# Exchanging two of the four first weight pieces between two DMA queues, one of them now between activation chunks

## The chip, the cores and the metric

The kernel runs on one core of one Trainium2 chip. The metric is the device time of one execution in microseconds (us); lower is better. All runs below are with a granted TensorE clock of 1.00. "Span" is the time that the profiler sees between the first and the last instruction; it is about 1.75 us shorter than the device time of the same run. In the profile PE is TensorE (matmuls and transposes), DVE is VectorE, ACT is ScalarE and POOL is GpSimd; "SP's queue" and "ScalarE's queue" hold the transfers that SyncE (SP) and ScalarE issue.

## The reference

The program is one transformer block of 2048 tokens by 1024 channels in bf16: a layer norm, an attention with 32 heads in four segments of 512 tokens, then a gated MLP. Only its first lines matter here:

```python
q = layernorm(x) @ wq ;  k = layernorm(x) @ wk ;  v = layernorm(x) @ wv
# then, per segment of 512 tokens: softmax(q k^T) v with a causal mask, plus a memory term; o @ wo; MLP
```

## The kernel before

Nothing can be computed until the first data have come, so the start of the kernel is laid out by hand. Segment 0 is four chunks of 128 tokens, x0 to x3 (256 KB each). The left half of `wv` is loaded in four pieces of 256 input rows (256 KB each), called pieces 0 to 3 here. V needs all four pieces; the pieces are consumed in the order of accumulation.

```python
for tc in range(4):
    x_load(tc)                       # SP queue: x0, x1, x2, x3
wv_piece(3, sp)                      # SP queue: piece 3
sp.dma_start(WK[:, :, 0:256], ...)   # then the other weights
# ... cut ...
for k in range(3):
    wv_piece(k, act)                 # ScalarE queue: pieces 0, 1, 2
```

In segment 0 the norm is done late. Chunks are only centered before the projection, V is scaled by 1/std when it leaves PSUM (the memory that TensorE writes its results to), and for Q and K the four chunks' 1/std are broadcast by TensorE (the tile `RSB`) and multiplied on. `act_mean` is a sum on ScalarE, `center` a subtraction on VectorE, `pe_Th` eight transposes on TensorE with two copies out of PSUM, `act_var` a sum of squares on ScalarE; `act_var` with its `rstd0`, and `aggr0`, each end in a pair of small GpSimd instructions. `v_pair(t, lo, hi)` is the V matmuls of chunk t with the 128-row blocks lo to hi, two blocks to a piece.

```python
v_pair(0, 0, 2)                 # chunk 0, piece 0
c1 = center(1, MEAN[1][:])
stats0(0, 0)
pe_Th(1, c1, dve, dve)
act_mean(2)                     # ScalarE: waits for x2
v_pair(0, 2, 4)                 # piece 1
v_pair(1, 0, 4)
v_pair(0, 4, 6)                 # piece 2
c2 = center(2, MEAN[2][:])
act_mean(3)                     # ScalarE: waits for x3
c3 = center(3, MEAN[3][:])
act_var(1)                      # chunk 1, but behind act_mean(2), act_mean(3) on ScalarE
rstd0(1)
stats0(0, 1)
aggr0(0)
pe_Th(2, c2, dve, act)
act_var(2)
rstd0(2)
v_pair(1, 4, 6)
v_pair(0, 6, 8)                 # piece 3
v_pair(1, 6, 8)
stats0(3, 0)
pe_Th(3, c3, dve, act)
stats0(3, 1)
aggr0(3)
# ... RSB; V of chunk 2; first K projection; TensorE broadcast of RSB; first Q projection ...
```

Of the kernel before, what the change touches and what calls it, by code (L numbers as in the profile page):

```python
# [257 lines left out]
def bass_sequential_preLN__memory_aug_infini_attn__mixer_gmlp__prompt_kernel(  # L258
# [17 lines left out]
    pe, act, dve, pool, sp = R.pe, R.act, R.dve, R.pool, R.sp  # L276
# [118 lines left out]
    def x_load(tc, eng=sp):  # L395
        eng.dma_start(XCH[tc % 4][:], x2d[tc * 128:(tc + 1) * 128, :])

    def wcols(ap, lo, hi):
        return ap[:, lo:hi].rearrange("(c p) n -> p c n", p=128)

    def wv_piece(k, eng):
        eng.dma_start(WV[0][:, 2 * k:2 * k + 2, :],
                      A_wv[k * 256:(k + 1) * 256, 0:512].rearrange("(c p) n -> p c n", p=128))

    for tc in range(4):
        x_load(tc)
    wv_piece(3, sp)
    sp.dma_start(WK[:, :, 0:256], wcols(A_wk, 0, 256))
    sp.dma_start(BETAB[:], A_beta.partition_broadcast(128))
    sp.dma_start(WQ[:, :, 0:256], wcols(A_wq, 0, 256))  # L410
# [7 lines left out]
    act.activation(RDM[:, 0, 0:1], MHALF[:], ACTF.Exp)  # L418
    pool.iota(IOT[:], [[1, 128]], base=0, channel_multiplier=-1)
    pool.memset(WV[0][:, 0, 0:16], 0.0)  # L420
    for k in range(3):
        wv_piece(k, act)
    pool.memset(V[:, :, :, 32:34], 1.0)
    pool.memset(BLK[:], 1.0)
# [509 lines left out]
    for tb in range(4):  # L934
# [9 lines left out]
        for tcl in range(4):  # L944
            tc = 4 * tb + tcl
# [38 lines left out]
```

## Time and profile before

| | before |
|---|---|
| device time | 795.58 us median of 3 (795.53 to 796.05) |
| span of the profiled run (a separate run of 796.20 us) | 794.5 us |
| TensorE busy | 784.4 us, 99% of the span |
| start of the first K projection | 13.98 us |
| start of the first Q projection | 16.16 us |

The first lines of the page give the span and the busy time of each engine (time, share, instructions):

```profile
span 794.5 us, 13030 instructions
...
PE 784.4 (99%) x5570; PEld 378.3 (48%) x5662; DVE 378.6 (48%) x741; ACT 296.7 (37%) x349; POOL 166.7 (21%) x329
```

TensorE is busy nearly always, so what can be won by moving loads lies in the start. The chain of waits, cut to the first 30 us, follows the last instruction back to what released it (start, duration, what):

```profile
0.79 0.91 ACT L209
...
1.74 6.50 DMA wv<-in_A_wv_dram
...
8.28 4.14 PE ps L209 x30
...
12.47 9.03 PE ps L209 x49
```

One load, a `wv` piece, is charged 6.50 us, and from its landing on TensorE runs almost without a stop. The timeline of TensorE shows what it did meanwhile (start, busy time, engine, source line, operation, output<-inputs, count; in brackets how long it was idle and what ended that):

```profile
6.78 0.62 PE L209 MATMUL ps<-ident,lno 128*128 128x128 bf16 x8
8.28 1.95 PE L209 MATMUL ps<-wv,xnT 128*128 128x512 bf16 x8 [0.88 <-DMA wv<-in_A_wv_dram]
10.07 0.61 PE L209 MATMUL ps<-ident,lno 128*128 128x128 bf16 x8
10.52 1.46 PE L209 MATMUL ps<-wv,xnT 128*128 128x512 bf16 x6
11.81 0.61 PE L209 MATMUL ps<-ident,lno 128*128 128x128 bf16 x8
12.47 1.67 PE L209 MATMUL ps<-wv,xnT 128*128 128x512 bf16 x7
13.98 1.89 PE L209 MATMUL ps<-xnT,wk 128*128 128x512 bf16 x8
15.71 0.61 PE L209 MATMUL ps<-ident,rsb 128*128 128x128 bf16 x8
16.16 1.89 PE L209 MATMUL ps<-xnT,wq 128*128 128x512 bf16 x8
```

The transposes of chunk 1 end at 7.40, then TensorE idles 0.88 us for piece 1. These are the lines the change was aimed at. "ident,lno" is a chunk's transposes, "xnT,wk" and "xnT,wq" the first K and Q projections, and "ident,rsb" the broadcast of the 1/std values. The GpSimd timeline shows their making, four pairs of instructions, of which the first and the very last instruction are shown:

```profile
10.70 0.19 POOL L209 TENSOR_SCALAR rs<-rs 128x1 f32<-128x1 f32 x1 [8.66 <-ACT junk L209]
...
13.90 0.56 POOL L209 TENSOR_TENSOR rsw<-rs,mhalf 128x1 f32<-128x1 f32 x1
```

The last ends at 14.46. On ScalarE the sum of x2 starts at 7.01:

```profile
7.01 1.06 ACT L209 ACTIVATE junk<-xch 128x1024 bf16<-128x1024 bf16 x1 [1.19 <-DMA xch<-in_A_x_dram]
...
9.38 1.15 ACT L209 ACTIVATE junk<-xch,mean 128x1024 bf16<-128x1024 bf16 x1
```

### The profile page before, as it was taken

How to read it: one execution, taken by the hardware profiler on the slowest of the kernel's cores; microseconds unless marked ns; L12 is line 12 of the kernel's file. 1: busy time of each engine (PE TensorE's matmuls, PEld its weight loads, DVE VectorE, ACT ScalarE, POOL GpSimd, SP SyncE). 2: the span in 40 equal slices, each digit the busy share in tenths (PEclk: the TensorE clock that was granted, in tenths of full speed). 3: DMA queues.
4: the chain of work that ended last, by engine and by line, in shares of the span. 5: the costliest groups of instructions: out<-in, count | busy, mean ns of one | idle time of the engine just before them, and what ended most of it. 6: DMA issues, size and time to landing. Idle time of an engine off the chain costs nothing.

```text
span 794.5 us, 13030 instructions
## 1 busy us (share of the span) xinstructions
PE 784.4 (99%) x5570; PEld 378.3 (48%) x5662; DVE 378.6 (48%) x741; ACT 296.7 (37%) x349; POOL 166.7 (21%) x329
## 2 busy tenths in 40 slices
PE   8999999999999999999999999999999999999998
PEld 3444455555554455455544444444444444444444
DVE  5585689579854766744561000053233323323332
ACT  6778877887787674233333333100000000000000
POOL 2665555556553331100230000000000000000000
PEclk9999999999999999999999999999999999999999
DMA  9544556364414425411116000740260143011002
GB/s 305 169 138 81 93 81 127 82 108 90 99 28 121 113 68 142 117 47 54 54 54 132 1 1 0 223 89 7 79 133 1 33 113 73 1 59 54 1 7 86
DMA packets 125002, 64.83 MB, mean 82 GB/s; under 512 B 94992, under 2 KB 113936, under 8 KB 124944
## 3 DMA queue, kind: packets, MB, share of 16 engines
q1 hardware_dynamic: 124128, 63.20, 32.9%
q8 instruction: 44, 0.72, 0.4%
q10 hardware_dynamic: 816, 0.79, 0.3%
q14 instruction: 14, 0.11, 0.0%
HBM read 32.51 MB, written 8.39 MB: 51 GB/s over the span
## 4 chain that ended last, share of the span: by engine, by line
PE 93%; DVE 5%; issue 1%; DMA 1%; ACT 0%; DVEq 0%
PE ps L209 93%; DVE stats L209 1%; DMA wv<-in_A_wv_dram 1%; DVE hch L209 1%; DVE otok L209 0%; DVE pqk L209 0%; DVE lno L209 0%; DVE ta L209 0%; DVE etmp L209 0%; DVE rd L209 0%; DVE mv L209 0%; DVE rdm L209 0%; ACT e L209 0%; ACT L209 0%; DVE upd L209 0%
## 5 line engine op out<-in xcount | busy, mean ns | idle before, releaser
L209 PE MATMUL ps<-wspT,z 128*128 128x512 bf16 x878 | 193.1, 379 | 0.9
L209 ACT ACTIVATE e<-ps 128x2048 bf16<-128x2048 f32 (+1 forms) x96 | 152.6, 1590 | 41.7 <-PE ps L209 41.5
L209 PEld LDWEIGHTS ps<-wspT,z 128*128 128x128 bf16 x896 | 87.7, 98 | 105.7
L209 DVE TENSOR_TENSOR tmpg<-ps,brow 128x512 f32<-128x512 f32 x56 | 38.7, 691 | 197.0 <-DMA brow<-in_B_b_sp_dram 104.0
L209 POOL TENSOR_SCALAR_AFFINE_SELECT e<-e 128x512 bf16<-128x512 bf16 x128 | 90.6, 720 | 132.4 <-ACT e L209 132.4
L209 PE MATMUL ps<-win,hnT 128*128 128x448 bf16 x512 | 98.3, 352 | 0.0
L209 PE MATMUL ps<-w_out,yT 128*128 128x512 bf16 (+2 forms) x453 | 96.9, 372 | 0.5
L209 PE MATMUL ps<-hnT,win 128*128 128x512 bf16 x439 | 96.2, 379 | 0.5
L209 PEld LDWEIGHTS ps<-win,hnT 128*128 128x128 bf16 x512 | 49.7, 98 | 46.4 <-issue 0.2
L209 PEld LDWEIGHTS ps<-w_out,yT 128*128 128x128 bf16 x462 | 44.7, 98 | 52.4
L209 PEld LDWEIGHTS ps<-hnT,win 128*128 128x128 bf16 x448 | 43.8, 98 | 52.8
L209 PE MATMUL ps<-xnT,wk 128*128 128x512 bf16 x233 | 59.6, 380 | 1.2
L209 PE MATMUL ps<-wv,xnT 128*128 128x512 bf16 x255 | 59.4, 380 | 1.2 <-DMA wv<-in_A_wv_dram 0.9
L209 ACT ACTIVATE z<-ps 128x448 bf16<-128x448 f32 x60 | 32.5, 543 | 69.4 <-PE ps L209 69.4
L209 PE MATMUL ps<-wo,oT 128*128 128x512 bf16 x254 | 57.7, 380 | 0.1
L209 ACT ACTIVATE z1T<-ps 128x512 bf16<-128x512 f32 x56 | 33.4, 597 | 63.3 <-PE ps L209 63.3
L209 DVE TENSOR_TENSOR fin<-fin,ps 128x512 bf16<-128x512 bf16 (+2 forms) x33 | 22.2, 672 | 71.2 <-DMA fin<-out_dram 38.7
L209 PE MATMUL ps<-xnT,wq 128*128 128x512 bf16 x226 | 54.0, 379 | 1.6
L209 DVE BATCH_NORM_STATS2 zst<-z 128x6 f32<-128x448 bf16 x64 | 38.9, 620 | 30.1 <-ACT z L209 30.1
L209 PEld LDWEIGHTS ps<-v,e 128*128 128x128 bf16 x1280 | 38.8, 96 | 14.0 <-issue 6.5
L209 PE MATMUL ps<-v,e 128*128 128x33 bf16 x1280 | 42.2, 178 | 0.0
L209 DVE TENSOR_TENSOR yT<-tmpg,z1T 128x512 bf16<-128x512 f32 x56 | 38.8, 692 | 1.9
(88 smaller groups left out, 603.9 us busy)
## 6 DMA issues: line engine op xcount, KB each, us to landing
xch<-in_A_x_dram SPq DMA_DIRECT2D x16, 256.0 KB, 3.7
xr<-in_A_x_dram SPq DMA_DIRECT2D x16, 256.0 KB, 4.0
out_dram<-hch SPq DMA_DIRECT2D x16, 256.0 KB, 2.4
fin<-out_dram SPq DMA_DIRECT2D x16, 256.0 KB, 2.8
out_dram<-fin SPq DMA_DIRECT2D x31, 128.0 KB, 1.7
win<-in_B_w_in_dram SPq DMA_DIRECT2D x4, 896.0 KB, 5.0
w_out<-in_B_w_out_dram SPq DMA_DIRECT2D x1, 3584.0 KB, 12.4
win<-in_B_w_in_dram SPq DMA_DIRECT2D x3, 1024.0 KB, 5.1
```

What stands on the lines that cost most here:

```text
L209: ins = getattr(e, op.name)(*op.args, **op.kw)
```

## The change

The intent is to have piece 1 earlier: it leaves ScalarE's queue, where it stood behind piece 0, and takes the third place on SP's queue, ahead of x2 and x3. In exchange piece 3 leaves SP's queue, and pieces 2 and 3 follow piece 0 on ScalarE's. The same bytes are moved by the same number of transfers.

```diff
-    for tc in range(4):
-        x_load(tc)
-    wv_piece(3, sp)
+    x_load(0)
+    x_load(1)
+    wv_piece(1, sp)
+    x_load(2)
+    x_load(3)
     sp.dma_start(WK[:, :, 0:256], wcols(A_wk, 0, 256))
 ...
-    for k in range(3):
+    for k in (0, 2, 3):
         wv_piece(k, act)
```

## The prediction

> **What bounds it now.** TensorE: 784.4 us busy of a span of 794.5 (the page, part 1), granted clock 1.00, and the chain of waits is 93% TensorE. In the first 30 us the chain names one load: 0.79 us of start-up, then 6.50 us of "DMA wv<-in_A_wv_dram" from 1.74 to 8.23, then TensorE almost without a gap until 24.8. The timeline: TensorE ends the transposes of x chunk 1 at 7.40 and starts the next V matmuls at 8.28, idle 0.88 us, waiting for the second w_v piece.
>
> **Landings before, us from the trace's semaphore records.** On SP's queue x0 3.7, x1 4.59, x2 6.93, x3 8.05, w_v piece 3 9.80; on ScalarE's queue pieces 0, 1, 2 at 5.11, 8.23, 9.58. Packets of both queues run in the same windows and move 300 to 380 GB/s together from 2.5 us on: they are full, so the change can only reorder bytes. The Trainium skill ("DMA: Bandwidth & Descriptors", section "Issuing engines are not separate DMA queues") says so: both queues interleave on the same 16 engines. Each gets about half.
>
> **What the change does.** It adds no bytes. Piece 1 is issued third on SP (about 1.72 us, against 1.74 on ScalarE before; an issue takes 0.40 to 0.49 us on either). It takes x2's place in SP's order; x2 takes x3's, x3 takes piece 3's; pieces 2 and 3 move up one place on ScalarE's. Estimates from the landings above: piece 1 at 6.9 (gain 1.3), piece 2 at 7.9, x2 at 8.0 (loss 1.1), x3 at 9.2 (loss 1.1), piece 3 at 9.6.
>
> **Critical path.** Piece 1 is then there before 7.40, so the 0.88 us idle should vanish; the eight V matmuls (0.22 us each) end near 9.2 instead of 10.07. But then the transposes of chunk 2 need its mean: x2 8.0, ScalarE sum 1.06 + 0.19, VectorE centering 0.49, so they start at 9.8, a new TensorE gap of about 0.6 us. Next, VectorE's centering of chunk 3 (9.38 before) goes to about 10.5, and behind it in program order the chunk 0 statistics and the chunk 2 copy (10.63 before, near 11.75 after). The V matmuls of chunk 2 need that copy: ready near 12.1, while TensorE reached them at 12.2 before. So of 0.88 us some 0.6 returns as the new gap and most of the rest in a second one. The first K projection (13.98 before) should start between 13.7 and 14.4. From there TensorE is full and carries the shift, about nothing, to the end. At most 0.3 us gained, at worst about 0.8 lost.
>
> **Predicted: 795.6 us, 794.9 to 796.5 (8 in 10). Faster by over 2%: 0; within 2%: 1.0; slower by over 2%: 0.** 2% is 16 us.
>
> **What would show it.** Right: no TensorE wait on wv near 8; one of 0.4 to 0.8 us for lno before the chunk 2 transposes; ScalarE's sum of x2 starting near 8.1, not 7.01; centering of chunk 3 later by about 1 us; K projection within 0.4 us of 13.98. Wrong: piece 1 landing after 7.4, or x2 landing before 7.4 (then up to 0.6 us is really gained).
>
> **What would make it wrong.** Arbitration that isn't even between queues (piece rows are 1 KB, x rows 2 KB); one slow DMA engine setting landings (piece 1's sixteen part landings spread from 6.26 to 8.23); x3 landing past 9.4, which delays everything behind its centering; and run-to-run spread, 0.5 us in three runs.

## The result

The changed kernel took 796.89 us (median of 4, 796.57 to 797.64), the kernel before 795.82 us (median of 4, 795.53 to 796.10). The ratio is 1.0015 with a 95% interval of 0.9998 to 1.0032. (The ratio and its interval are taken from the fast runs themselves, and are not quite the ratio of the medians quoted.) By the threshold of 2% that is the same time. But it lies above the predicted range, and the experiments show where the loss comes from, and that it is mostly smaller than in these four runs.

The page of the changed kernel, same lines:

```profile
span 795.9 us, 13122 instructions
...
PE 789.8 (99%) x5662; PEld 378.2 (48%) x5662; DVE 378.7 (48%) x741; ACT 296.7 (37%) x349; POOL 167.2 (21%) x329
```

(TensorE's busy sum is not comparable to a few microseconds: the earlier trace has 5570 matmul records, this one 5662, so some were missing there.) The chain of waits no longer goes through a `wv` piece but through an x chunk, and it now visits every engine:

```profile
2.18 7.05 DMA xch<-in_A_x_dram
...
9.32 1.16 ACT junk L209 x2
...
10.50 1.16 ACT junk L209 x2
...
11.69 0.49 DVE lno L209
...
13.94 0.24 POOL rs L209
...
14.26 0.57 POOL rsw L209
...
16.14 0.57 POOL rsw L209
...
16.73 0.18 DVE rsb L209
...
17.16 12.85 PE ps L209 x86
```

It reads: x2 lands at 9.23; ScalarE sums x2, then x3; VectorE centers chunk 3; statistics; the GpSimd pairs; the `rsb` cast; and only at 17.16 does TensorE broadcast 1/std. (One step of it is doubtful, see below.) TensorE's timeline, line for line as before:

```profile
6.64 0.62 PE L209 MATMUL ps<-ident,lno 128*128 128x128 bf16 x8
8.21 1.90 PE L209 MATMUL ps<-wv,xnT 128*128 128x512 bf16 x8 [0.94 <-DMA wv<-in_A_wv_dram]
11.05 0.62 PE L209 MATMUL ps<-ident,lno 128*128 128x128 bf16 x8 [0.94 <-DVE lno L209]
11.50 1.46 PE L209 MATMUL ps<-wv,xnT 128*128 128x512 bf16 x6
12.80 0.61 PE L209 MATMUL ps<-ident,lno 128*128 128x128 bf16 x8
13.36 1.90 PE L209 MATMUL ps<-wv,xnT 128*128 128x512 bf16 x8
15.10 1.89 PE L209 MATMUL ps<-xnT,wk 128*128 128x512 bf16 x8
17.16 0.62 PE L209 MATMUL ps<-ident,rsb 128*128 128x128 bf16 x8 [0.17 <-DVE rsb L209]
17.61 1.89 PE L209 MATMUL ps<-xnT,wq 128*128 128x512 bf16 x8
```

Three waits are to be seen. In this run the one for piece 1 is still there (0.94 us). A new one of 0.94 us stands before the transposes of chunk 2 ("<-DVE lno"). And another, labelled 0.17 us, stands before the broadcast of `rsb`. The last is worth more than its label, since the label counts from the modelled end of the last matmul: from the start of the K projection to that of the broadcast it is 17.16 - 15.10 = 2.06 us here, and 15.71 - 13.98 = 1.73 us before. GpSimd and ScalarE show why it is there:

```profile
13.02 0.19 POOL L209 TENSOR_SCALAR rs<-rs 128x1 f32<-128x1 f32 x1 [10.97 <-ACT junk L209]
...
16.14 0.56 POOL L209 TENSOR_TENSOR rsw<-rs,mhalf 128x1 f32<-128x1 f32 x1
```

```profile
9.32 1.06 ACT L209 ACTIVATE junk<-xch 128x1024 bf16<-128x1024 bf16 x1 [3.25 <-DMA xch<-in_A_x_dram]
...
11.68 1.15 ACT L209 ACTIVATE junk<-xch,mean 128x1024 bf16<-128x1024 bf16 x1
```

GpSimd's first pair waited for the variance of chunk 1. That needs neither x2 nor x3, but stands behind both of their sums in ScalarE's program order. So the variance started at 11.68 instead of 9.38, and the last of the four pairs ended at 16.70 instead of 14.46. The chain of waits names VectorE's statistics before the second pair (13.94), but GpSimd was busy with the first pair until 13.86, and the statistics that the second pair needs were ready at 13.02. In experiment 6 below, where the first pair goes earlier, the second starts at 11.98, while the statistics named here run on until 12.78. So it was the first pair that held it.

When each load landed is in the trace's semaphore records. A load counts as landed when the last of its sixteen parts has arrived. In us, with the median of the sixteen parts in brackets:

| | x2 | x3 | piece 1 | piece 2 | piece 3 |
|---|---|---|---|---|---|
| before | 6.93 (5.70) | 8.05 (7.34) | 8.23 (6.41) | 9.58 (8.27) | 9.80 (8.59) |
| changed | 9.23 (7.17) | 10.37 (8.49) | 8.16 (5.85) | 8.42 (6.34) | 10.59 (8.48) |

By the median part the queues did what was asked: pieces 1 and 2 came 0.56 and 1.93 us earlier, x2 and x3 1.47 and 1.15 later. But a tile is usable only with its last part, and in this run that came about 2 us behind the median part from the third transfer on (8.16 - 5.85 = 2.31, 9.23 - 7.17 = 2.06, 10.37 - 8.49 = 1.88). Two of the sixteen parts were late each time (piece 1's at 7.31 and 8.16, x2's at 8.54 and 9.23, x3's at 9.66 and 10.37), the other fourteen had landed by 6.74, 7.78 and 9.08. That looks like one or two DMA engines that fell behind and stayed behind, but it isn't shown, since the records don't name the engine.

The Trainium skill ("DMA: Bandwidth & Descriptors", section "Why a DMA increments its semaphore by 16 and not by 1") says that a transfer runs on up to sixteen engines that finish independently and that only the full count means that all has landed. The trace agrees: sixteen part landings per load, spread over as much as 2.8 us for piece 1 (5.37 to 8.16) and 3.2 us for piece 3 (7.43 to 10.59).

### The profile page after: what moved, and what is told of

Same layout as the page of the kernel before. It is cut to its first block, busy times and chain, and to the rows that moved or that the text cites. A ratio compares the mean times of both kernels' runs of the same rounds, so it can differ in the third digit from the quotient of the medians.

```text
span 795.9 us, 13122 instructions
## 1 busy us (share of the span) xinstructions
PE 789.8 (99%) x5662; PEld 378.2 (48%) x5662; DVE 378.7 (48%) x741; ACT 296.7 (37%) x349; POOL 167.2 (21%) x329
## 4 chain that ended last, share of the span: by engine, by line
PE 98%; DMA 1%; DVE 0%; POOL 0%; ACT 0%; SPq 0%; issue 0%; ACTq 0%
PE ps L209 98%; DMA xch<-in_A_x_dram 1%; ACT junk L209 0%; POOL rsw L209 0%; SPq L209 0%; DVE stats L209 0%; POOL rs L209 0%; DVE lno L209 0%; DVE rsb L209 0%; DVE fin L209 0%; DVE xnT L209 0%; DVE mv L209 0%; ACTq L208 0%
## 5 line engine op out<-in xcount | busy, mean ns | idle before, releaser
L209 PE MATMUL ps<-xnT,wq 128*128 128x512 bf16 x256 | 60.5, 379 | 0.0
```

What stands on the lines that cost most here:

```text
L209: ins = getattr(e, op.name)(*op.args, **op.kw)
```

## The experiments

Twelve kernels ran, each five times, in three sessions on three chips (1 to 4, 5 to 8, 9 to 12), beside nine runs of the kernel before in each session. All passed the comparison with the reference, also the two that compute something wrong (experiments 2 and 7), whose error it doesn't see.

One measure made a difference of half a microsecond readable. In all fourteen traces (before, changed, twelve experiments) the span minus the start of the first Q projection is 778.25 to 778.34 us. So whatever these kernels differ in, and also what one run differs from another, arose before the first Q projection. Its start, called Q here, is the number to explain.

Theory X: x2 and x3 lose a place on SP's queue, and their chain through ScalarE, VectorE and GpSimd then holds TensorE. Rival W: the `wv` pieces in their new places hold it. Rival S: it is chance in the slowest DMA engine, and the order costs nothing.

### 1. The changed kernel again

The loops are written out; the instructions are the same.

> The changed kernel, again, for its time over five rounds and for a second trace. Theory X (x chunks 2 and 3 land one place later and the chunk 2 and 3 chain then holds TensorE): 0.6 to 1.3 us slower than before, x2 landing after 8.0, first K projection starting 14.6 to 15.2. Rival S (the profiled run only caught a slow DMA engine; the order costs nothing): times within 0.3 us of before, first K projection near 14.0.

Measured: 796.73 us (796.15 to 797.12), before 796.36 (795.67 to 796.55), ratio 1.0004 (0.9991 to 1.0018). x2 landed at 8.48, piece 1 at 7.42, Q was 16.84. TensorE's timeline:

```profile
7.47 1.90 PE L209 MATMUL ps<-wv,xnT 128*128 128x512 bf16 x8
10.29 0.62 PE L209 MATMUL ps<-ident,lno 128*128 128x128 bf16 x8 [0.93 <-DVE lno L209]
...
16.39 0.62 PE L209 MATMUL ps<-ident,rsb 128*128 128x128 bf16 x8 [0.15 <-DVE rsb L209]
```

This time the wait for piece 1 is gone (the V matmuls start at 7.47). The waits for lno and rsb are there again. So those two belong to the change; the wait for piece 1 in the first trace came of its late last part. The time lies 0.37 us above before by the medians and the first K projection started at 14.34: both fall between what theory X said (0.6 to 1.3, 14.6 to 15.2) and what rival S said (within 0.3, near 14.0), and the interval doesn't exclude a difference of zero.

### 2. Nothing early waits for x2 and x3 (wrong result)

The transfers stay as in the change. The norm's early work on chunks 2 and 3 reads chunks 0 and 1:

```diff
-    act_mean(2)
+    act_mean(2, 0)              # reads XCH[0] in place of XCH[2]
-    c2 = center(2, MEAN[2][:])
+    c2 = center(2, MEAN[2][:], src=0)
# ... the same for act_var(2) and, with chunk 1's data, for chunk 3 ...
```

> The changed kernel with the first norm's work on chunks 2 and 3 reading chunks 0 and 1 instead (wrong result on purpose), so nothing early waits for x2 and x3; all transfers stay. Theory X: the 0.94 us TensorE wait for lno and the later centering of chunk 3 go, first K projection at 13.7 to 14.2, time within 0.3 us of before or up to 0.4 below. Rival W (the w_v pieces in their new places are what holds TensorE): the loss stays, K projection near 15, time 0.6 to 1.3 above before.

Measured: 795.32 us (794.98 to 795.47) against 796.36, ratio 0.9988 (0.9975 to 1.0000). Q was 14.93. TensorE no longer stops between the V matmuls and Q:

```profile
7.07 1.94 PE L209 MATMUL ps<-wv,xnT 128*128 128x512 bf16 x8
8.84 0.61 PE L209 MATMUL ps<-ident,lno 128*128 128x128 bf16 x8
...
12.75 1.89 PE L209 MATMUL ps<-xnT,wk 128*128 128x512 bf16 x8
14.48 0.61 PE L209 MATMUL ps<-ident,rsb 128*128 128x128 bf16 x8
14.93 1.89 PE L209 MATMUL ps<-xnT,wq 128*128 128x512 bf16 x8
```

Without the x chain the moved pieces are worth 1.04 us against the kernel before (medians) and 1.41 us against the changed kernel. That is more than expected. Here neither piece sets Q any more: by the sums derived below, piece 1 (6.80) would give 14.73 and piece 2 (7.64) 14.22, and the chain of waits goes back to x0. Rival W falls: with the same transfers, it is the dependence on x2 and x3 that makes the change lose.

### 3. Displacement alone

```diff
-    x_load(2); x_load(3); wv_piece(3, sp)
+    wv_piece(3, sp); x_load(2); x_load(3)      # ScalarE keeps pieces 0, 1, 2
```

> Displacement alone: SP carries x0, x1, piece 3, x2, x3 and ScalarE pieces 0, 1, 2 as before, so x2 and x3 lose a place but piece 1 gains nothing. Theory X: x2 lands 8.0 to 9.3, as slow as the change (0.6 to 1.3 us above before). Rival W: x is harmless, time within 0.3 us of before.

Measured: 796.19 us (796.06 to 796.57) against 796.36, ratio 1.0000 (0.9987 to 1.0012). A miss for the size in theory X: no loss is seen in the times, which by themselves fit rival W's forecast here. The trace says that the mechanism was there all the same: x2 landed at 8.19, the chain of waits runs through x2, ScalarE and GpSimd to `rsb` as in the changed kernel, and Q was 16.55, 0.39 later than in the trace of before. With x2 at 8.2 the chain is hardly longer than what TensorE waited for pieces 1 and 2 anyway. The cost is not a fixed number; it is the difference of two nearly equal paths.

### 4. Piece 1 on SP, x2 in its old place on ScalarE's queue

```diff
-    x_load(2); x_load(3); wv_piece(3, sp)       # SP, behind x0 and x1
+    wv_piece(1, sp); x_load(3); wv_piece(3, sp)
-    wv_piece(0, act); wv_piece(1, act); wv_piece(2, act)
+    wv_piece(0, act); x_load(2, act); wv_piece(2, act)
```

> Piece 1 in SP's third place, as in the change, but x2 takes piece 1's old place on ScalarE's queue and x3 and piece 3 stay where they were. Theory X: x2 lands about 8.2 (one and a quarter late, not two), x3 8.0 as before, piece 2 at 9.6 as before and therefore still the gate of the fifth V matmul of chunk 0; K projection 13.9 to 14.5, time between before and 0.6 above. If an early piece 1 is worth something by itself: up to 0.5 us below before.

Measured: 795.92 us (795.84 to 796.46) against 796.36, ratio 0.9998 (0.9985 to 1.0010). x2 landed at 7.33, x3 at 8.70, piece 2 at 8.88, Q was 15.87. It is no loss, and by the medians a gain of 0.44 that the interval doesn't confirm. The chain goes through x3 here, so this version too ends on the x chain. The landings were misjudged: x2 was expected near 8.2, piece 2 at 9.6 and the first K projection at 13.9 or later; it started at 13.38.

### 5. The kernel before again

The loop is written out; the instructions are the same.

> The kernel before, written out differently, instruction for instruction the same: for a second trace of it and for the size of the noise. Time within 0.4 us of the runs of before beside it. From the traces so far, span minus start of the first Q projection is 778.25 to 778.34 in every kernel, so all differences arise before it. Expected here: Q projection start 15.6 to 16.5, set by the w_v pieces (piece 1's landing + 7.9), and 778.3 again.

Measured: 796.23 us (795.73 to 796.41) against 796.31 (795.92 to 796.63) for the same program in the same session. The ratio is 0.9998 (0.9986 to 1.0011), which is what nothing looks like here. Q was 16.19. In this trace the chain ran through piece 2 (landed at 9.61), not piece 1. In the first trace of before both give the same Q, so an early piece 1 alone could not have gained: piece 2 stood right behind it.

### 6. The changed kernel with the variance of chunk 1 moved forward

```diff
+    act_var(1)
+    rstd0(1)
     act_mean(2)
     ...
     c3 = center(3, MEAN[3][:])
-    act_var(1)
-    rstd0(1)
```

> The changed kernel with the variance sum of chunk 1 (ScalarE) and its rsqrt (GpSimd) moved in program order ahead of the sum of chunk 2, which waits for x2. Theory X2 (after the change the path runs x2, two ScalarE sums, the variance of chunk 1 queued behind them, then four rsqrt pairs back to back on GpSimd, then the TensorE broadcast of them): GpSimd's first pair starts near 7.4, no TensorE wait for rsb, Q projection at x2's landing + 7.9 instead of + 8.36, time 0.3 to 0.6 us below the changed kernel. If only the transposes of chunk 2 matter: no change of time beyond 0.2.

Measured: 796.17 us (795.82 to 796.39) against 796.31, ratio 0.9998 (0.9986 to 1.0011). x2 landed at 8.12 and Q was 16.15, that is 8.03 after it, against 8.38, 8.36 and 8.36 in the three traces of the changed kernel. GpSimd's first pair, and TensorE:

```profile
7.11 0.19 POOL L209 TENSOR_SCALAR rs<-rs 128x1 f32<-128x1 f32 x1 [5.07 <-ACT junk L209]
```

```profile
9.93 0.62 PE L209 MATMUL ps<-ident,lno 128*128 128x128 bf16 x8 [0.47 <-DVE lno L209]
...
15.70 0.61 PE L209 MATMUL ps<-ident,rsb 128*128 128x128 bf16 x8
```

The pair starts at 7.11, the wait for `rsb` is gone, and from K to the broadcast it is 1.72 us, as before the change. The wait for lno stays, as it must with x2 late. So the order of one ScalarE instruction behind two sums it doesn't need was worth 0.33 us. The ratio to before is 0.06% lower than in experiment 1; that comparison goes across two sessions.

### 7. The kernel before, not waiting for x2 and x3 (wrong result)

The edit of experiment 2 on the kernel before.

> The kernel before with the first norm's work on chunks 2 and 3 reading chunks 0 and 1 (wrong result on purpose). Theory X: before the change x2 and x3 are in good time (x2's landing 6.93 + 8.36 is 15.3, the w_v pieces give 16.1), so nothing changes: Q projection 15.6 to 16.5, time within 0.3 us of before. If the reading of other chunks speeds things by itself: 0.5 us or more below, and then e2_nox proves less.

Measured: 796.25 us (795.94 to 796.65) against 796.31, ratio 1.0000 (0.9988 to 1.0013), Q 15.89. Before the change the x chain is off the path, and the edit by itself gains nothing. That makes experiment 2 count.

### 8 and 11. The kernel before with another TensorE order

```diff
-    v_pair(0, 2, 4)
-    v_pair(1, 0, 4)
-    v_pair(0, 4, 6)
+    v_pair(1, 0, 2)             # needs piece 0 only
+    v_pair(0, 2, 4)
+    v_pair(1, 2, 4)
     ...
     pe_Th(2, c2, dve, act)
+    v_pair(0, 4, 6)
```

> The kernel before, transfers unchanged, with TensorE's order changed: chunk 1's first two V matmuls, which need only piece 0, go ahead of the wait for piece 1, and the transposes of chunk 2 ahead of the matmuls of piece 2. Theory: fills about 0.45 us of the 0.88 us wait, Q projection at about 15.7, time 0.3 to 0.5 us below before. If the wait merely moves to piece 2 (9.58): within 0.15 us of before.

> e8_peorder again, for a second trace and more spans: the earlier transfers with TensorE's reordered start. Expected 0.4 to 0.7 us below before, Q projection 15.3 to 16.0.

Measured: 795.62 us (795.35 to 796.24) against 796.31, ratio 0.9994 (0.9981 to 1.0008), Q 15.41; and again 795.90 us (795.55 to 796.19) against 796.11 (795.37 to 796.96), ratio 0.9998 (0.9985 to 1.0010), Q 15.77. From the first of the two traces:

```profile
7.59 1.47 PE L209 MATMUL ps<-wv,xnT 128*128 128x512 bf16 x6 [0.30 <-DVE xnT L209]
8.89 0.61 PE L209 MATMUL ps<-ident,lno 128*128 128x128 bf16 x8
...
15.41 1.89 PE L209 MATMUL ps<-xnT,wq 128*128 128x512 bf16 x8
```

The wait for piece 1 is filled with work that was ready. Q is 0.4 to 0.8 us earlier than in the two traces of before; the times lie 0.69 and 0.21 us below it by the medians, and both intervals hold 1. The gain of the second run is smaller than expected (0.4 to 0.7).

### 9. The changed kernel a third time

The kernel of experiment 1.

> The changed kernel a third time, for a third trace and five more spans beside the repaired versions. Expected: 0.3 to 0.9 us above before; Q projection at x2's landing + 8.36, x2's last part landing 8.2 to 9.2, a TensorE wait for rsb of 0.1 to 0.2. If a fourth of its runs are as fast as before's median, the loss is mostly one of chance in the slowest DMA engine.

Measured: 796.41 us (796.08 to 796.58) against 796.11, ratio 1.0003 (0.9990 to 1.0015). x2 landed at 8.14, Q was 16.50. Of its five runs two (796.08 and 796.11) reach before's median of 796.11, more than a fourth, so by the mark set beforehand the loss is mostly one of chance in the slowest DMA engine. The chain itself is there: x2 landed just before the expected 8.2 to 9.2, and Q is its landing + 8.36, as expected.

### 10. The changed kernel, repaired

Experiment 6, and the two matmuls of chunk 1 with piece 2 go ahead of the wait for chunk 2:

```diff
     v_pair(0, 4, 6)
+    v_pair(1, 4, 6)
     ...
     pe_Th(2, c2, dve, act)
     ...
-    v_pair(1, 4, 6)
```

> The changed kernel, repaired for late x chunks: variance of chunk 1 ahead of the sum of chunk 2 (as in e6_var1), and two V matmuls of chunk 1 with piece 2 ahead of the transposes of chunk 2, to fill the wait for them. Theory: Q projection at x2's landing + 7.5, that is 15.7 to 16.2, time 0.2 to 0.6 us below before.

Measured: 796.26 us (795.85 to 796.81) against 796.11, ratio 1.0001 (0.9987 to 1.0015). A miss. x2 landed at 8.59 and Q was 16.62, 8.03 after it and not 7.5. The time saved before the chunk 2 transposes came back one step later: TensorE then waited 0.38 us for the copy of chunk 2, which stands behind the centering of chunk 3 in VectorE's order, and that waits for ScalarE's sum of x3. It is the step that the prediction had named as "a second one". The wait on TensorE's timeline:

```profile
12.71 1.90 PE L209 MATMUL ps<-wv,xnT 128*128 128x512 bf16 x8 [0.38 <-DVE xnT L209]
```

### 12. Transfers in the order of need

```diff
-    x_load(2); x_load(3); wv_piece(3, sp)
+    x_load(2); wv_piece(1, sp); x_load(3)       # ScalarE: pieces 0, 2, 3
```

The TensorE order is that of experiment 8, with `v_pair(1, 4, 6)` still directly after `v_pair(0, 4, 6)`; `act_var(1)`, `stats0(0, 1)`, `aggr0(0)` and `pe_Th(2)` go ahead of chunk 3's centering.

> All repairs together, transfers in the order of need with x2 kept third on SP's queue (x0, x1, x2, piece 1, x3; ScalarE: pieces 0, 2, 3), variance of chunk 1 and statistics of chunk 0 ahead of chunk 3's work, transposes of chunk 2 ahead of chunk 3's centering. Theory: x2 lands near 6.8 and is off the path; TensorE waits only briefly for pieces 1 and 2 near 8.0; Q projection 15.2 to 15.8, time 0.5 to 1.0 us below before. If x3, now last on SP's queue (9.3 to 9.9), gates: Q above 16.

Measured: 795.82 us (795.76 to 796.42) against 796.11, ratio 0.9998 (0.9985 to 1.0010). x2 landed at 6.68, off the path as meant. The profiled run was the slowest of the five (796.42): piece 1, now fourth on SP's queue, landed at 8.95, its last part 1.37 us behind the median one, and Q was 16.39, above its expectation. The expectation had x3 as what could bring Q above 16; the chain of waits runs through piece 1 and not x3 (9.85). By the medians it is 0.29 us below before, less than the expected 0.5 to 1.0.

### The traces together

With the program order of the kernel before, each load has a shortest way to Q: piece 1's landing + 7.93, piece 2's + 6.58, x2's + 8.36, x3's + 7.17. The first two numbers are read off the first trace of before (16.16 - 8.23 and 16.16 - 9.58), the third off experiment 1 (16.84 - 8.48), the fourth off experiment 4 (15.87 - 8.70). The largest sum should be Q. Landings and Q in us:

| trace | piece 1 | piece 2 | x2 | x3 | largest sum | Q |
|---|---|---|---|---|---|---|
| before | 8.23 | 9.58 | 6.93 | 8.05 | pieces 1 and 2: 16.16 (read off) | 16.16 |
| before, exp. 5 | 8.09 | 9.61 | 6.77 | 7.87 | piece 2: 16.19 | 16.19 |
| before without x, exp. 7 | 7.78 | 9.31 | no wait | no wait | piece 2: 15.89 | 15.89 |
| changed | 8.16 | 8.42 | 9.23 | 10.37 | x2: 17.59 | 17.61 |
| changed, exp. 1 | 7.42 | 7.69 | 8.48 | 9.62 | x2: 16.84 (read off) | 16.84 |
| changed, exp. 9 | 7.02 | 7.78 | 8.14 | 9.30 | x2: 16.50 | 16.50 |
| displaced, exp. 3 | 7.99 | 9.66 | 8.19 | 9.27 | x2: 16.55 | 16.55 |
| swapped, exp. 4 | 7.57 | 8.88 | 7.33 | 8.70 | x3: 15.87 (read off) | 15.87 |

Five rows are not fitted, and they come out within 0.02 us. The change takes the two `wv` sums down (by about 0.1 to 1.2 us for piece 1 and 1.2 to 1.9 for piece 2) and puts x2's sum, which had 0.87 us to spare (16.16 - 6.93 - 8.36), above where they were.

How large is the loss? The changed kernel's 14 runs have a mean of 796.64 us, the 31 runs of the kernel before 796.17: 0.5 us, or 0.06%. That pools three chips and one session in which the changed kernel didn't run; each of the three intervals by itself holds 1. In the three sessions with both, the difference of the means is 1.2, 0.43 and 0.20 us. In the traces, what differs from one to the next is how late x2's last part came. Rival S is thus partly right about the size and wrong about the cause: all three traces of the changed kernel have the x2 chain on the path and neither of the two traces of before does.

## Why the prediction was wrong

It said 795.6 us with a range of 794.9 to 796.5; 796.89 was measured. Point by point:

- **What bounds the kernel, and that bytes are only reordered: right.** Experiment 2 shows that the wait for the pieces is worth about a microsecond, and experiment 7 that x was off the path. In the trace of before, half-microsecond windows from 2.5 to 9.5 us moved 291 to 381 GB/s, and from 4 to 8 us ScalarE's queue had 0.48 of the bytes of both queues ("about half").
- **"Piece 1 at 6.9 (gain 1.3), piece 2 at 7.9, x2 at 8.0 (loss 1.1), x3 at 9.2": right in order, off in size.** Over three traces of the change: piece 1 8.16, 7.42, 7.02; piece 2 8.42, 7.69, 7.78; x2 9.23, 8.48, 8.14; x3 10.37, 9.62, 9.30. So x2 was 1.23, 0.48 and 0.14 us later than predicted. The prediction took the last-part landings of one trace as a property of the place in the queue. By the median part x2 came at 7.17 to 7.55, where x3 had been (7.34); the last part follows at up to 2.06 us. The prediction's own list of risks names this (one slow DMA engine, x3 past 9.4), but its sum doesn't allow for it.
- **The 0.88 us wait for piece 1 vanishes: right in experiments 1 and 9, not in the first trace.**
- **A new wait for the centering of chunk 2, about 0.6 us: right.** 0.94, 0.93 and 0.45 us. ScalarE's sum of x2 started at 9.32, 8.57 and 8.22 (predicted 8.1).
- **"The first K projection should start between 13.7 and 14.4": right in two of three.** 15.10, 14.34, 14.00.
- **"From there TensorE is full and carries the shift, about nothing, to the end": this step failed.** K to Q took 2.18 us before and 2.51, 2.50 and 2.50 after. The prediction followed the late x2 as far as V of chunk 2 and stopped there. It did not follow the second branch: the variances, with chunk 1's queued on ScalarE behind the sums of x2 and x3, then four pairs of GpSimd instructions back to back (13.02 to 16.70 in the changed kernel), then the broadcast before Q. With x2 at the predicted 8.0 this branch gives Q = 8.0 + 8.36 = 16.36, 0.20 above before; with x2 as it landed, 0.34 to 1.45 above.
- **How much each is worth.** Experiment 6, without the second branch, has Q at x2 + 8.03. So the path that the prediction did follow gives 16.03 with x2 at 8.0, 0.13 below before, which is its "about nothing". The branch it left out adds 0.33 us, in every trace; the late landing adds 1.23, 0.48 and 0.14. Together that is 1.43, 0.68 and 0.34, where 1.45, 0.68 and 0.34 were measured. In the first trace, then, most of the miss is the mis-sized landing of x2. That size varies from run to run, so it was partly bad luck that the result fell so far outside: the means of the three sets of runs are 797.00, 796.65 and 796.34, and the last lies inside the predicted range. (The 8.03 is from one trace.)
- **The range was too narrow.** "Run-to-run spread, 0.5 us in three runs" was taken for the noise. The 31 runs of the kernel before go from 795.37 to 796.96.

## What to carry to other kernels

When a load is moved forward, something else moves back: for each displaced transfer, sum its way to the point where all paths meet, through every engine's program order, not only to the next wait on the busiest engine. Look on that way for instructions that need nothing late but stand behind some that do; moving one such variance forward took away 0.33 us. And where a step waits for whole tiles, reckon with the slowest of sixteen parts, from several traces.

The versions that look better than both kernels keep x2 from being last in the race, by another order of transfers or of work (experiments 4, 8, 11, 12: 0.2 to 0.7 us below before by the medians). None is clear of the noise with five or ten runs. Why the last part of a load falls so far behind in some runs, and whether the changed order makes that likelier, stays open.

## What the Trainium skill lacked or had wrong

- "DMA: Bandwidth & Descriptors", section "Why a DMA increments its semaphore by 16 and not by 1", has the sixteen parts, but not how far apart they land with the queues full: here 256 KB loads ended 0.13 to 2.31 us after their median part (third place on SP's queue, fourteen traces). Nor does the page say that a lag can last over several transfers: in the changed kernel's first trace 2.31, 2.06 and 1.88 us in three transfers in a row. It doesn't always: in experiment 8's trace piece 1 came 1.41 us after its median part, and x3, whose median part came next, 0.28.
- The same page, section "Issuing engines are not separate DMA queues", says that issuing from several engines only saves the issue time. For the sum of the bytes that fits (345 GB/s of both queues together from 2.5 to 9.5 us before, 328 in the changed kernel's first trace). For the order of arrival that section says nothing (other parts of the page treat the order within a queue, without a size): which queue a piece stands on, and behind what, moved the median part of piece 2 by 1.93 us (8.27 to 6.34).
- The same page, section "Specifications", gives about 0.6 us to the first byte for both hardware queues. On SP's queue the first packet came 0.62 us after the end of the first issue (0.80 + 0.40 to 1.82), which agrees. On ScalarE's queue, issued while SP's transfers were under way, it came 1.60 us after in the trace of before (1.25 + 0.45 to 3.30), and 1.26 to 1.96 us after over the fourteen traces.
